# A linear attention and two feed-forward stages on one core: four small hand-overs between engines, a different order of preparation, and fewer fill products

## The chip, the cores and the metric

The kernel runs on one core of a Trainium2 chip. The metric is the device time of one execution in microseconds; the median of the runs counts. Five engines take part: TensorE (PE in the rows, PEld for its weight loads), VectorE (DVE), ScalarE (ACT), GpSimd (POOL), and SyncE (SP), which issues almost all DMAs.

## The reference

Three stages follow one another: a gated linear recurrence per batch and head, a feed-forward layer with a rational function of h, and a second feed-forward layer with a softmax-weighted, normalised h.

```python
for t in range(S):                       # B, H, S, D = 4, 8, 768, 48
    state = alpha[:, :, t, :, None] * state + einsum('bhd,bhe->bhde', k[:, :, t], v[:, :, t])
    y[:, :, t] = einsum('bhd,bhde->bhe', q[:, :, t], state)
h = x @ w_in                             # 3072 x 384, d_ff 2048
g = (a0 + a1*h + a2*h2 + a3*h3) / (1 + |b0||h| + |b1|h2 + 1e-6)
x = g @ w_out
h = x @ w_in                             # d_ff 1024
solu = h * softmax(h); out = layernorm(solu) * g_ln @ w_out
```

## The kernel before, in words

**Precision.** Every operand of the feed-forward products is split in two: `hi` is a copy rounded to float32r, `lo` the remainder, and each product is done three times (hi·hi, hi·lo, lo·hi).

**Halves.** The 768 steps are six chunks of 128. A chunk has two halves of two batches each; they are numbered 0 to 11 here, so the fourth half has the index 3 and the fifth the index 4. In a half the running product P of alpha and its inverse R are taken; q is multiplied by P and k by R; TensorE then forms the scores (`sc`, line 433), which ScalarE copies out of PSUM and GpSimd masks (lines 441, 442), the output `y` (458), and the state update `u` (498). At lines 485 and 486 y is split into the hi and lo parts of `xt`, the input of the first feed-forward layer: ScalarE copies hi, VectorE subtracts for lo.

**Preparing a half.** Halves 0 and 1 are prepared by `a_turn`: TensorE transposes alpha, k and q into PSUM (375), VectorE scans (386, 390) and multiplies k (394) and q (395). From half 2 on `a_dve` does it: VectorE transposes (302, 307, 336), scans (320, 329) and multiplies k (332), GpSimd multiplies q (347); the result goes out to HBM and comes back in another layout (`a_move_qk`, line 288). It is a generator with six steps.

**Units.** The first feed-forward layer is cut into 96 units, 16 per chunk (128 of its 2048 columns, 512 tokens). `m_up(u)` has nine products into a PSUM tile `hp` (line 607, three buffers, so unit u+3 waits until unit u is done with its tile), then a chain on ScalarE and VectorE (with `MIX` also on GpSimd: lines 625 to 631; without: 632 to 638). The last VectorE instruction of a unit is remembered as `fin[u]`. ScalarE makes `gh` (640), GpSimd `gl` (641). `m_down(u)`, four units later, has nine products into `x2p` (653). Of a unit with MIX VectorE has three instructions and GpSimd two more than without, where VectorE has four.

**Weights.** `w1_group(n)` loads and unpacks the float64 weights of units 4n to 4n+3 (and their second-layer rows) in seven steps; each step is one DMA, three VectorE instructions (552, 555, 556), one copy on ScalarE (562) and one subtraction on GpSimd (563). Groups 0 and 1 run ahead of the units, in buffers lent from later tiles; group 2 runs two steps per unit from unit 0, group 3 from unit 4.

**Order.** The order is written in the loop over u (from line 906): weights, fill products, `m_up(u)`, one step of the half in progress (`side`), `m_down(u-4)`. A planner orders the instructions of each engine by this program; `issue_after(x)` puts what it encloses behind instruction x in that order. `half_steps(i)` runs the scores, outputs and state update of half i (`a_pe`), one step per unit, and beside it two steps per unit of the preparation of half i+1, both behind `fin[u-2]` (`pin`, GP = GS = 2). A side is begun every eight units, at the units 2, 10, 18, ... (`LATE`).

**Fill products.** `busy(n, ins)` puts n bfloat16 products of zeros behind an instruction on TensorE (line 240). 66 of them lie at six places, 24 of these ahead of unit 3.

Of the kernel before, what the change touches and what calls it, by code (L numbers as in the profile page):

```python
# [7 lines left out]
F32 = mybir.dt.float32  # L8
# [22 lines left out]
def kernel(  # L31
# [32 lines left out]
    BUSY = {(0, 0): 14, (0, "kp", 1): 12, (1, 0): 4, (1, 1): 4, (1, "y"): 8, 3: 24}  # L64
# [15 lines left out]
    MIX = lambda u: u < 24 and u % 2 == 0  # L80
# [73 lines left out]
    def network(fast):  # L154
# [7 lines left out]
        if fast:  # L162
# [9 lines left out]
            zero = ap_.tile([128, CH], BF16, name="zero")  # L172
            nc.vector.memset(zero, 0.0)
# [3 lines left out]
            d1 = ap_.tile([128, NB6 * PER + 1], BF16, name="d1")  # L177
            d2 = ap_.tile([128, NB6 * PER], F32, name="d2")
# [6 lines left out]
        def clear():  # L185
            nc.gpsimd.memset(d1, 0.0)
            nc.gpsimd.memset(_view(d1[:], 0, [[PER, NB6 + 1]]), 1.0)
            nc.gpsimd.memset(d2, 0.0)
            nc.vector.memset(alT[:, 0:1], 0.0)
# [34 lines left out]
        halves = {}  # L224

# [6 lines left out]
        if fast:  # L232
            none = _view(zero[:], 0, [[0, NTOK // CH], [1, CH]])

        def busy(n, ins):
            if not spare:
                spare.append(ps_x2p.tile([128, NTOK], F32, name="spare", tag="x2p2"))
            with tc.issue_after(ins.ins):
                for _ in range(n):
                    nc.tensor.matmul(spare[0], lhsT=zero, rhs=none, start=True, stop=True)  # L240
# [124 lines left out]
        def a_turn(i):  # L365
# [15 lines left out]
            for p in range(2):  # L381
# [13 lines left out]
                marks[i, p, 0] = nc.vector.tensor_tensor(hf.q[p], turn(rq, p), P, ALU.mult)  # L395
# [28 lines left out]
        def a_pe(i):  # L424
# [58 lines left out]
            for z, n in enumerate((2, 1)):  # L483
                hi, lo = (xt[:, 2 * z:2 * z + n, w, 256 * bp:256 * bp + 256] for w in range(2))
                nc.scalar.activation(hi, y2[z], AF.Copy)
                marks[i, z] = nc.vector.tensor_tensor(lo, y2[z], hi.bitcast(F32), ALU.subtract)
# [35 lines left out]
        def split_w(src, hi, lo, scale=None):  # L522
# [16 lines left out]
            if src.dtype == I64:  # L539
# [8 lines left out]
                nc.sync.dma_start(out=st[:, :n], in_=src)  # L548
# [311 lines left out]
        def pin(n):  # L860
            stack = ExitStack()
            if n <= now[0] < NU and fast:
                for e, u in (("PE", now[0]), ("ACT", now[0] - n), ("POOL", now[0] - n)):
                    stack.enter_context(tc.issue_after(last[e, u].ins))
# [3 lines left out]
        def half_steps(i):  # L868
            gp = a_pe(i)
            gd = chain(a_prep(i + 1), a_move_qk(i + 1) if i + 1 >= NPE else iter(()), a_load(i + 2, ("ra", "rk")) if i + 2 < NH and i + 1 >= NPE else iter(())) if i + 1 < NH else iter(())  # L870
            while True:
                with pin(GP):
                    a = next(gp, "end")
                with pin(GS):
                    b = next(gd, "end")
                    if b != "end":
                        b = next(gd, "end")
                if a == "end" and b == "end":
# [11 lines left out]
        for u in range(NU + LAG):  # L890
            c, f = divmod(u, NF1)
            now[0] = u
            if f % (NF1 // 2) == LATE and u < NU:
# [3 lines left out]
            if u < NU:  # L897
# [7 lines left out]
                if fast and u < NF1:  # L905
# [6 lines left out]
                    with later(G1):  # L912
                        take(prep, 1)
# [3 lines left out]
                if fast and u < NF1:  # L917
                    with later(G1):
                        take(prep, 1)
# [157 lines left out]
```

## Time and profile before

| | us |
|---|---|
| median of 3 runs (lowest to highest) | 781.32 (779.75 to 789.72) |
| the profiled execution | 778.25 |
| span of its trace | 776.5 |
| TensorE, VectorE, ScalarE, GpSimd busy in the span | 737.9, 634.6, 534.1, 356.2 |
| mean granted clock of TensorE | 0.984 |

The times of the rows below are from the start of the span of the profiled execution. A granted clock of 1.00 is 2.4 GHz, of 0.50 1.2 GHz; a value between is a mean over a stretch with both.

### The profile page before, as it was taken

How to read it: one execution, taken by the hardware profiler on the slowest of the kernel's cores; microseconds unless marked ns; L12 is line 12 of the kernel's file. 1: busy time of each engine (PE TensorE's matmuls, PEld its weight loads, DVE VectorE, ACT ScalarE, POOL GpSimd, SP SyncE). 2: the span in 40 equal slices, each digit the busy share in tenths (PEclk: the TensorE clock that was granted, in tenths of full speed). 3: DMA queues.
4: the chain of work that ended last, by engine and by line, in shares of the span. 5: the costliest groups of instructions: out<-in, count | busy, mean ns of one | idle time of the engine just before them, and what ended most of it. 6: DMA issues, size and time to landing. Idle time of an engine off the chain costs nothing.

```text
span 776.5 us, 14048 instructions
## 1 busy us (share of the span) xinstructions
PE 737.9 (95%) x5042; PEld 605.7 (78%) x5042; DVE 634.6 (82%) x1110; ACT 534.1 (69%) x983; POOL 356.2 (46%) x306
## 2 busy tenths in 40 slices
PE   6788898999999999999999999999999999999996
PEld 4655676778887787778877788888888989989986
DVE  5999999999898989899898966568887697867630
ACT  2337856688878888788878887878865555555541
POOL 3256886577554355434444433422253333442322
PEclk9989997999999999999999999999999999999998
DMA  7997257376837383727545340820025353442552
GB/s 175 271 267 185 69 157 163 116 178 184 201 125 159 116 199 94 155 81 214 128 141 100 123 82 2 320 87 1 1 82 116 106 138 89 123 106 55 139 124 71
DMA packets 87278, 101.74 MB, mean 131 GB/s; under 512 B 34464, under 2 KB 63136, under 8 KB 87200
## 3 DMA queue, kind: packets, MB, share of 16 engines
q1 hardware_dynamic: 87104, 100.67, 49.2%
q8 instruction: 41, 0.67, 0.4%
q14 instruction: 37, 0.30, 0.1%
q10 hardware_dynamic: 96, 0.10, 0.0%
HBM read 60.59 MB, written 27.56 MB: 114 GB/s over the span
## 4 chain that ended last, share of the span: by engine, by line
PE 35%; DVE 20%; ACT 9%; issue 4%; DMA 2%; POOL 1%; SPq 1%; ACTq 0%; DVEq 0%; POOLq 0%
PE h L727 10%; PE op L791 9%; PE x2p L653 8%; PE hp L607 7%; DVE hp L637 2%; DVE p L633 2%; DVE w L636 2%; ACT hp L635 2%; DVE P L320 1%; DVE p L638 1%; DVE alT L336 1%; DVE room L767 1%; DVE qk L302 1%; ACT p L614 1%; ACT gh L640 1%
## 5 line engine op out<-in xcount | busy, mean ns | idle before, releaser
L607 PE MATMUL hp<-xt,g 128*128 128x512 f32 x864 | 222.5, 399 | 5.8 <-DVE alT L314 2.4
L641 POOL TENSOR_TENSOR gl<-p,gh 128x512 fp32r<-128x512 f32 x96 | 129.1, 1345 | 194.2 <-ACT gh L640 104.7
L653 PE MATMUL x2p<-gh,g 128*128 128x512 f32 x576 | 197.1, 396 | 2.1 <-ACT x2e L661 2.1
L607 PEld LDWEIGHTS hp<-xt,g 128*128 128x128 f32 x864 | 161.7, 190 | 45.7 <-DVE p L638 5.8
L653 PEld LDWEIGHTS x2p<-gh,g 128*128 128x128 f32 x576 | 108.0, 188 | 29.0 <-ACT x2e L661 4.7
L653 PE MATMUL x2p<-gl,g 128*128 128x512 f32 x288 | 113.7, 395 | 1.2 <-POOL gl L641 1.2
L791 PE MATMUL op<-w2oh,room 128*128 128x384 f32 x384 | 101.8, 339 | 1.5 <-ACT room L782 0.9
L783 POOL TENSOR_TENSOR room<-room,room 128x1024 fp32r<-128x1024 f32 x22 | 54.6, 2485 | 101.1 <-ACT room L782 96.6
L636 DVE SCALAR_TENSOR_TENSOR w<-w,co,hp 128x512 f32<-128x512 f32 x84 | 62.0, 738 | 42.0 <-ACT hp L635 41.0
L727 PE MATMUL h<-w2ih,x 128*128 128x512 f32 x288 | 90.8, 394 | 0.0
L614 ACT ACTIVATE p<-hp,co 128x512 f32<-128x512 f32 x96 | 65.9, 686 | 14.0 <-POOL gl L641 13.6
L635 ACT ACTIVATE hp<-ah 128x512 f32<-128x512 f32 x84 | 50.2, 597 | 33.9 <-DVE p L633 32.9
L791 PEld LDWEIGHTS op<-w2oh,room 128*128 128x128 f32 x384 | 70.1, 188 | 3.0 <-ACT room L782 1.2
L633 DVE SCALAR_TENSOR_TENSOR p<-p,co,hp 128x512 f32<-128x512 f32 x84 | 61.7, 734 | 10.4 <-ACT p L614 10.0
L615 ACT ACTIVATE w<-ah,co 128x512 f32<-128x512 f32 x96 | 69.4, 723 | 0.6 <-DVE p L631 0.2
L612 ACT ACTIVATE ah<-hp 128x512 f32<-128x512 f32 x96 | 56.6, 590 | 13.1 <-PE hp L607 12.6
L653 PEld LDWEIGHTS x2p<-gl,g 128*128 128x128 f32 x288 | 54.4, 189 | 13.9 <-POOL gl L641 1.6
L791 PE MATMUL op<-w2ol,room 128*128 128x384 f32 x192 | 65.0, 339 | 0.0
L640 ACT ACTIVATE gh<-p 128x512 fp32r<-128x512 f32 x96 | 59.9, 624 | 6.6 <-PE x2p L653 2.7
L727 PEld LDWEIGHTS h<-w2ih,x 128*128 128x128 f32 x288 | 53.9, 188 | 11.7
L638 DVE SCALAR_TENSOR_TENSOR p<-p,co,hp 128x512 f32<-128x512 f32 x84 | 62.0, 738 | 1.1
L634 ACT ACTIVATE ah<-w,co 128x512 f32<-128x512 f32 x84 | 60.6, 721 | 1.3
(170 smaller groups left out, 1281.1 us busy)
## 6 DMA issues: line engine op xcount, KB each, us to landing
room<-room SPq DMA_DIRECT2D x96, 128.0 KB, 2.3
qk_d<-qk SPq DMA_DIRECT2D x10, 771.0 KB, 4.9
st<-in_moe_w_in_dram SPq DMA_DIRECT2D x13, 512.0 KB, 4.7
st<-in_moe_w_out_dram SPq DMA_DIRECT2D x16, 384.0 KB, 4.5
qks<-qk_d SPq DMA_DIRECT2D x20, 257.0 KB, 5.1
x<-x_d SPq DMA_DIRECT2D x18, 256.0 KB, 3.2
out_dram<-o SPq DMA_DIRECT2D x94, 48.0 KB, 1.6
ra<-in_alpha_dram SPq DMA_DIRECT2D x44, 96.0 KB, 3.4
```

The lines of the kernel that those rows point to most:

```text
L607: last["PE", u] = nc.tensor.matmul(hp, lhsT=w[:, kt, 128 * o:128 * o + 128], rhs=xts[c][:, kt, xx, :], start=(kt == 0 and w is hi and xx = ...
L614: nc.scalar.activation(p, hp, AF.Square, bias=co[:, 7:8])
L615: nc.scalar.activation(w, ah, AF.Square, bias=co[:, 6:7])
L633: nc.vector.scalar_tensor_tensor(p, p, a1, hp, ALU.add, ALU.mult)
L635: nc.scalar.activation(hp, ah, AF.Exp, scale=-1.0)
L636: nc.vector.scalar_tensor_tensor(w, w, rest, hp, ALU.add, ALU.mult)
L638: fin[u] = nc.vector.scalar_tensor_tensor(p, p, a0, hp, ALU.add, ALU.mult)
L640: last["ACT", u] = nc.scalar.activation(gh, p, AF.Copy)
L641: last["POOL", u] = nc.gpsimd.tensor_tensor(gl, p, gh[:].bitcast(F32), ALU.subtract)
L653: nc.tensor.matmul(x2ps[c][d], lhsT=w[:, o, 128 * d:128 * d + 128], rhs=gg, start=(f == 0 and w is hi and gg is gh), stop=(f == NF1 - 1 an ...
L727: nc.tensor.matmul(hp[:, 512 * n:512 * n + 512], lhsT=x2s[c][:, kt, x, CH * b:CH * b + CH], rhs=w2[w][:, kt, 512 * n:512 * n + 512], start ...
L791: nc.tensor.matmul(op, lhsT=x[:, 128 * f:128 * f + 128], rhs=w2[w][:, f, :], start=(f == 0 and x is hi and w == "oh"), stop=(f == NF2 - 1 ...
```

## The change

It does the following. The q products of halves 0 and 1 go from one VectorE instruction each to a ScalarE copy out of PSUM and a GpSimd product. The lo part of y in halves 0 to 3 is formed by TensorE, which adds minus hi to y in PSUM (a product with a negated identity), and ScalarE copies the result. Units 0 and 2 lose MIX. The preparation of half 3 is held until unit 4 and that of half 4 until unit 13; the side of half 4 begins at unit 20 in place of 18. Group 2 takes no step in unit 0 and is put behind `fin[u-1]` in units 1 to 3; while `near` holds its loads are put behind the last load of group 1. The fill products become 50, 12 of them ahead of unit 3, and read the tile `d1`, which is now filled at the start and also gives the zeros of the scans.

```diff
-    BUSY = {(0, 0): 14, (0, "kp", 1): 12, (1, 0): 4, (1, 1): 4, (1, "y"): 8, 3: 24}
+    HOLD = {2: (4, 2), 3: (13, 2)}
+    BUSY = {(0, 0): 10, (0, "kp", 1): 8, (1, 0): 8, (1, 1): 8, (1, "y"): 4, 3: 12}
...
-    MIX = lambda u: u < 24 and u % 2 == 0
+    MIX = lambda u: 2 < u < 24 and u % 2 == 0
...
-            zero = ap_.tile([128, CH], BF16, name="zero")
-            nc.vector.memset(zero, 0.0)
+            minus = ap_.tile([128, 128], F32R, name="minus")
+            nc.scalar.activation(minus, ident, AF.Copy, scale=-1.0)
...
             d1 = ap_.tile([128, NB6 * PER + 1], BF16, name="d1")
+            nc.gpsimd.memset(d1, 0.0)
+            nc.gpsimd.memset(_view(d1[:], 0, [[PER, NB6 + 1]]), 1.0)
+            zero = d1[:, 1:1 + CH]
...
-            none = _view(zero[:], 0, [[0, NTOK // CH], [1, CH]])
+            none = d1[:, :NTOK]
...
-                    nc.tensor.matmul(spare[0], lhsT=zero, rhs=none, start=True, stop=True)
+                    nc.tensor.matmul(spare[0], lhsT=none[:, :128], rhs=none, start=True, stop=True)
...
-                marks[i, p, 0] = nc.vector.tensor_tensor(hf.q[p], turn(rq, p), P, ALU.mult)
+                nc.scalar.activation(hf.q[p], turn(rq, p), AF.Copy)
+                marks[i, p, 0] = nc.gpsimd.tensor_tensor(hf.q[p], hf.q[p], P, ALU.mult)
...
                 nc.scalar.activation(hi, y2[z], AF.Copy)
-                marks[i, z] = nc.vector.tensor_tensor(lo, y2[z], hi.bitcast(F32), ALU.subtract)
+                if i < NPE + 2:
+                    for a in range(n):
+                        nc.tensor.matmul(
+                            y2[z][:, a, :], lhsT=minus, rhs=hi[:, a, :], start=False, stop=True, skip_group_check=True
+                        )
+                    marks[i, z] = nc.scalar.activation(lo, y2[z], AF.Copy)
+                else:
+                    marks[i, z] = nc.vector.tensor_tensor(lo, y2[z], hi.bitcast(F32), ALU.subtract)
...
-                nc.sync.dma_start(out=st[:, :n], in_=src)
+                with tc.issue_after(sent["w"].ins) if stage["near"] else ExitStack():
+                    move = nc.sync.dma_start(out=st[:, :n], in_=src)
+                if stage["wide"]:
+                    sent["w"] = move
...
-                with pin(GS):
-                    b = next(gd, "end")
-                    if b != "end":
+                b = None
+                if now[0] >= HOLD.get(i, (0, 0))[0]:
+                    with pin(HOLD.get(i, (0, GS))[1]):
                         b = next(gd, "end")
+                        if b != "end":
+                            b = next(gd, "end")
...
-            if f % (NF1 // 2) == LATE and u < NU:
+            if f % (NF1 // 2) == (4 if u // (NF1 // 2) == 2 else LATE) and u < NU:
...
-                    with later(G1):
-                        take(prep, 1)
+                    with later(1 if u < 4 else G1):
+                        take(prep, 1 if u else 0)
```

The last pair stands twice, ahead of `m_up(u)` and behind it. `pin` takes the unit before where `m_up(u)` has not been written yet.

## Rows read from the trace of the kernel before

**Rows 1.** The page, busy time of each engine, share of the span, instructions

```profile
PE 737.9 (95%) x5042; PEld 605.7 (78%) x5042; DVE 634.6 (82%) x1110; ACT 534.1 (69%) x983; POOL 356.2 (46%) x306
```

**Rows 2.** Busy time by stretch: length, engines, TensorE clock, DMA share, GB/s

```profile
20.00:40.00 20.00, 16.02 (x207) 12.20 (x204) 19.53 (x56) 6.74 (x15) 6.75 (x8) 0.91 1.04 276
...
100.00:150.00 50.00, 45.33 (x388) 35.37 (x391) 48.66 (x71) 31.41 (x59) 35.48 (x31) 0.90 0.57 150
...
450.00:500.00 50.00, 50.00 (x366) 40.92 (x365) 32.38 (x46) 41.42 (x72) 16.87 (x17) 1.00 0.35 106
```

**Rows 3.** Chain that ended last, in order of time: nine of a unit's eighteen products

```profile
451.25 2.04 PE hp L607 x9
```

**Rows 4.** TensorE's timeline, first transposes, units 0, 3, 5, half 3's scores, unit 16

```profile
4.50 1.98 PE L375 MATMUL tp<-ident,ra 128*64 128x128 f32 x16 [4.50 <-POOL d L187]
...
55.20 1.04 PE L607 MATMUL hp<-xt,g 128*128 128x512 f32 x3
...
74.35 2.33 PE L607 MATMUL hp<-xt,g 128*128 128x512 f32 x9 [2.40 <-DVE alT L314]
...
85.35 2.34 PE L607 MATMUL hp<-xt,g 128*128 128x512 f32 x9 [1.03 <-DVE p L631]
...
120.62 2.03 PE L433 MATMUL sc<-qks 48*128 48x128 f32 x8 [1.70 <-DVE alT L314]
...
159.26 2.21 PE L607 MATMUL hp<-xt,g 128*128 128x512 f32 x9
```

**Rows 5.** VectorE's timeline, q products of halves 0 and 1 among others

```profile
16.56 0.69 DVE L395 TENSOR_TENSOR qks<-tp,Pp 128x512 f32<-128x512 f32 x1
17.61 0.69 DVE L552 TENSOR_SCALAR fp<-lent 128x512 int32<-128x512 int32 x1 [0.37 <-DMA lent<-in_moe_w_in_dram]
...
36.32 0.65 DVE L395 TENSOR_TENSOR lent<-tp,Pp 128x512 f32<-128x512 f32 x1
36.89 0.53 DVE L556 SCALAR_TENSOR_TENSOR ft<-lent,fp 128x384 int32<-128x384 int32 x1
```

**Rows 6.** Timelines of ScalarE and GpSimd: a copy from PSUM, an SBUF pair

```profile
43.28 0.58 ACT L441 ACTIVATE A<-sc 128x512 f32<-128x512 f32 x1
...
49.75 1.28 POOL L563 TENSOR_TENSOR g<-ft,g 128x512 fp32r<-128x512 f32 x1
```

**Rows 7.** The two splits of y of half 1: VectorE, then ScalarE

```profile
56.80 1.01 DVE L486 TENSOR_TENSOR xt<-y,xt 128x512 fp32r<-128x512 f32 x2
...
53.76 0.87 ACT L485 ACTIVATE xt<-y 128x512 fp32r<-128x512 f32 x2 [0.24 <-PE y L458]
```

**Rows 8.** VectorE's timeline up to the end of unit 0

```profile
63.89 0.71 DVE L552 TENSOR_SCALAR fp<-st 128x512 int32<-128x512 int32 x1
...
73.02 0.68 DVE L556 SCALAR_TENSOR_TENSOR ft<-lent,fp 128x512 int32<-128x512 int32 x1
73.61 0.68 DVE L631 SCALAR_TENSOR_TENSOR p<-w,hp 128x512 f32<-128x512 f32 x1
```

**Rows 9.** Instructions on tile alT, then on tile qk: length, VectorE, others

```profile
120.00:152.00 32.00, 10.01 (x10) 0.84 0.54 139
...
120.00:152.00 32.00, 7.40 (x13) 0.39 (x2) 0.41 (x1) 0.84 0.54 139
```

**Rows 10.** DMA issues from 0 to 60 us: KB each, us to landing

```profile
lent<-in_moe_w_out_dram SPq DMA_DIRECT2D x8, 384.0 KB, 6.3
```

**Rows 11.** TensorE's timeline: fill products at two granted clocks

```profile
49.34 1.89 PE L240 MATMUL spare<-zero 128*128 128x512 bf16 x4
...
68.75 3.20 PE L240 MATMUL spare<-zero 128*128 128x512 bf16 x14
```

**Rows 12.** GpSimd's timeline: the q product of half 3

```profile
105.72 1.82 POOL L347 TENSOR_TENSOR qk<-qk,P 128x768 f32<-128x768 f32 x1
```

**Rows 13.** VectorE's groups from 0 to 161 us: busy, mean ns

```profile
L555 DVE SCALAR_TENSOR_TENSOR ft<-st,ft 128x384 int32<-128x384 int32 (+1 forms) x7 | 7.0, 994 | 0.0
L555 DVE SCALAR_TENSOR_TENSOR fp<-st,fp 128x512 int32<-128x512 int32 (+1 forms) x10 | 6.4, 640 | 0.1
```

More of the change, by code (lines that the diff above doesn't have):

```diff
@@ L185, in clear @@
         def clear():
-            nc.gpsimd.memset(d1, 0.0)
-            nc.gpsimd.memset(_view(d1[:], 0, [[PER, NB6 + 1]]), 1.0)
             nc.gpsimd.memset(d2, 0.0)
@@ L224, in network @@
         halves = {}
+        sent = {}
         def half(i):
@@ L862, in pin @@
             if n <= now[0] < NU and fast:
-                for e, u in (("PE", now[0]), ("ACT", now[0] - n), ("POOL", now[0] - n)):
+                for e, u in (("PE", now[0] if ("PE", now[0]) in last else now[0] - 1), ("ACT", now[0] - n), ("POOL", now[0] - n)):
                     stack.enter_context(tc.issue_after(last[e, u].ins))
@@ L917, in network @@
                 if fast and u < NF1:
-                    with later(G1):
-                        take(prep, 1)
+                    with later(1 if u < 4 else G1):
+                        take(prep, 1 if u else 0)
             if u == NU:
```

## The prediction

> **What bounds the kernel now.** I read the page's busy times first, then the table by stretch, then the timelines of TensorE and VectorE up to 160 us. Over the whole span TensorE is busy 95% and VectorE 82% [rows 1], which hides two different stages. From 450 us on TensorE is busy 50.00 of 50 us while VectorE has 32.38 [rows 2]: TensorE is the bound, and a unit takes 2.04 + 2.04 = 4.08 us [rows 3]. In front it is the other way round: VectorE is busy 19.53 of 20 us between 20 and 40, and 48.66 of 50 between 100 and 150, where TensorE has 45.33 and a granted clock of 0.90 [rows 2]. Unit 0 begins at 55.20 and unit 16 at 159.26 [rows 4], so sixteen units take 104.1 us; at 4.08 each they need 65.3, beside the products of two halves of attention. Unit 3 stands for 2.40 us until VectorE's memset at line 314, which lies directly behind the end of unit 0, and unit 5 for 1.03 until unit 2 ends [rows 4]. So up to unit 16 what VectorE has to do sets the time, and from there TensorE. A microsecond that leaves VectorE's queue ahead of unit 16, or is put behind it, brings unit 16 forward by about one; after it nothing is gained.
>
> **The change part by part, as microseconds by which unit 16 comes earlier.**
>
> *q products.* Four VectorE instructions go. The next instruction starts 0.57 us after the one at 36.32 [rows 5], so 0.6 each, 2.4 in all. Behind the one at 16.56 VectorE waits 0.37 us for a weight DMA anyway [rows 5], so part of half 0's two is lost. Bounds 1.2 (half 1 alone) and 2.4; I take 1.8, the middle, since half 0 loses only a part. In their place come four ScalarE copies, by the copy of scores 0.58 us each, and four GpSimd products, by the subtraction of the same size 1.28 us each [rows 6]; in 20 to 40 us these engines are busy 6.74 and 6.75 of 20 [rows 2], and the copy does not have to wait for P, so both lie beside VectorE's scan and k product. Uncovered, half 1's chain would be longer by 0.58 + 1.28 − 0.65 = 1.2 us.
>
> *y splits.* VectorE gives up 0.6 + 0.35 = 0.95 us by the starts of the next instructions (0.68 and 0.41 by duration), and 0.92 at 56.80 [rows 7]: 1.9 for halves 0 and 1, and as much for halves 2 and 3, which also lie ahead of unit 16: 3.8. In place of it TensorE gets three products of 256 columns, by half of 2.04/9 us [rows 3] 0.34 us a half, which stand behind ScalarE's copy (0.87 us for two [rows 7]); then ScalarE copies twice more, 0.9 us. TensorE works its queue in order, so up to 0.87 + 0.34 = 1.2 us of it per half may be lost; in a stretch bound by VectorE that costs nothing, and I take nothing (bounds 0 and 4 × 1.2 = 4.8, the upper one only if nothing lies between). For half 1 it is even shorter: hi is ready at 54.63 and VectorE comes to lo at 56.80 only.
>
> *MIX off for units 0 and 2.* One VectorE instruction more each, of 0.68 us by the last of unit 0 [rows 8]: −1.3 (0 to −1.4). GpSimd loses two instructions per unit.
>
> *Group 2 behind unit 0.* Between 63.89 and 73.02 seven VectorE instructions of group 2, 0.6 us each, stand ahead of the end of unit 0 at 74.29 [rows 8]. They only move behind it, 4.2 us, so unit 0 ends near 74.3 − 3.7 − 4.2 + 0.7 = 67.1, and units 3 to 5 come earlier, but by unit 8 group 2 has to be there. As a sum over VectorE that is nothing. What it can cost: the step's DMA goes behind the same mark, and a load of this kind takes 6.3 us to land [rows 10]. With half 3's preparation held as well, VectorE may run dry there. Bounds 0 and −6.3; I take −2, nearer to 0, because the chains of units 1 and 2 lie ready. SP's order changes for these loads alone; behind them stand the reads of half 3's inputs, which are wanted later than before.
>
> *Half 3 from unit 4.* Moved, not removed, and its result is still wanted at unit 10: 0 here, and a rival below.
>
> *Half 4 from unit 13.* Its preparation is 10.01 + 7.40 us of VectorE, less about 2.6 for two lines that touch both tiles, 14.8 us, all of it between 120 and 152 [rows 9], that is ahead of unit 16. Held until unit 13, steps 1 and 2 stand behind the end of unit 11, 3 and 4 behind unit 12, 5 and 6 behind unit 13, and unit 16 waits for the end of unit 13 (three hp buffers). So the last two steps, about a quarter (3.7 us), surely fall behind it, and at most about 12 do. I take 6: the last two, and half of the two before. Unit 32 needs half 4, so the moved work has 16 units in which to be done, and the side of half 5 moves with it.
>
> *Fill products.* At full clock one takes 3.20/14 = 0.23 us, at 1.2 GHz 1.89/4 = 0.47 [rows 11]. Ahead of unit 3 twelve go (2.7 us), but TensorE stood 2.40 us behind them [rows 4], so nothing is gained. In half 1 eight are added and four go, +0.9 us at full clock, +1.9 at half, on the way from the scores to y; the larger number of them may in turn end the low clock earlier. Bounds −2 and +2, taken as 0.
>
> *Sum:* 1.8 + 3.8 − 1.3 − 2 + 6 = 8.3 us. Against the profiled execution: span 776.5 − 8.3 = 768.2, time 778.25 − 8.3 = 770.0. The median of the runs is 3.07 above that execution; 781.3 − 8.3 = **773.0 us**.
>
> **A rule against the change.** Line 555 takes 994 ns on average where both its inputs lie in SBUF, and 640 where one is in PSUM [rows 13]; GpSimd is at work beside both. The Trainium skill, page "SBUF — State Buffer", section "SBUF: two separate sides", says that VectorE, in an instruction with two SBUF inputs, and GpSimd share a pair of ports which one holds for its whole instruction while the other stands still. The trace agrees in the 994 against 640. The four new GpSimd products read SBUF. As a mechanism of this kernel: if VectorE stood still through each of them, 4 × 1.28 = 5.1 us come off, 8.3 − 5.1 = 3.2, and the time is 778.1. Against it: in halves 0 and 1 the scans, the k product and the unpacking of weights each read one operand from PSUM, so I give it a small chance.
>
> **The rivals.**
>
> *The order gives nothing.* If the planner or the waits let half 4's work be done ahead of unit 16 all the same, 6 us go: 8.3 − 6 = 2.3, 779.0 us. For it: VectorE's ready work is taken up wherever it waits a moment. Against: the pins are written out.
>
> *All of it moves, and no load is waited for.* 12 in place of 6, 0 in place of −2: 16.3, 765.0 us. For it: TensorE loses more than that ahead of unit 16 (104.1 against 65.3 and the attention). Against: steps 1 to 4 may run ahead of unit 13's end.
>
> *Half 3 comes too late (slower).* Its q product ends at 107.5 [rows 12], then its data go out to HBM and back, and at 120.62 the scores already stand 1.70 us on TensorE [rows 4], ahead of unit 11 in the queue. Now it starts behind unit 2's end in place of unit 0's: by the starts of units 5 and 3, 85.35 − 74.35 = 11.0 us later [rows 4]. If the whole of that comes through, −8.3 + 11.0 = +2.7, 784.0 us. It decides from where that product ends later than 107.5 + 8.3 = 115.8. Against it: group 2's and the units' work that stood beside it is then behind it no more, and VectorE's sum up to its end is the same or less.
>
> **How the numbers follow.** Forecast 0.45, order gives nothing 0.22, all moves 0.16, half 3 late 0.12, ports 0.05. The range from 764 to 784 holds the sum's own bounds and nearly all of the rivals; outside lie part of the 765 case (more than 16 us) and part of the late case (with a low clock on top), together under 0.2. The forecast's own range is 768 to 778. 2% is 15.6 us, about what a measurement of this kernel can tell from no change. Below 765.7 lies most of the third case: 0.13 for faster. Above 796.9 would need the late half twice over: 0.02. Between: 0.85.
>
> **What would show it.** Right: unit 0 begins near 51.5 in place of 55.20, unit 3 near 65 to 68, unit 16 near 151; VectorE's line 395 is gone and 486 begins with half 4; the scans of half 4 (lines 320 and 329) lie around the start of unit 16; behind unit 16 the distances between units are as before. Wrong: unit 16 within 3 us of 159; half 3's q product later than 115.8 and TensorE idle ahead of its scores; VectorE idle for more than 4 us between units 0 and 4 on weight loads; granted clock 0.5 for longer ahead of unit 16 than before, with TensorE waiting for nothing; or new TensorE gaps at the halves behind unit 20.

## The result, and the profile after

| | before | after |
|---|---|---|
| median of 16 runs each, us (lowest to highest) | 781.36 (777.0 to 789.72) | 791.08 (789.8 to 792.51) |
| ratio to before, 95% interval | | 1.0123 [1.0103, 1.0143] |
| profiled execution, span, us | 778.25, 776.5 | 792.39, 790.5 |
| mean granted clock | 0.984 | 0.976 |

The changed kernel is 9.7 us slower where 773.0 was forecast: outside the range, and with the other sign. The page of after, first line, answers to [rows 1]:

```profile
PE 740.8 (94%) x5033; PEld 610.6 (77%) x5038; DVE 631.5 (80%) x1099; ACT 539.3 (68%) x996; POOL 352.7 (45%) x306
```

VectorE does 3 us less, as meant. The next look is TensorE's timeline at four of the places of [rows 4]: first transposes, units 0, 3 and 16.

```profile
4.47 1.97 PE L378 MATMUL tp<-ident,ra 128*64 128x128 f32 x16 [4.47 <-POOL d L180]
...
65.15 0.86 PE L621 MATMUL hp<-xt,g 128*128 128x512 f32 x3
...
82.92 1.65 PE L621 MATMUL hp<-xt,g 128*128 128x512 f32 x3 [4.77 <-DVE p L652]
...
165.97 0.39 PE L621 MATMUL hp<-xt,g 128*128 128x512 f32 x1
```

The start is the same, unit 0 is 10.0 us late, unit 3 8.6, unit 16 6.7. Unit 32 begins at 251.0 in place of 241.2, and from there to unit 95 the lateness stays at 9.9. All of the loss lies ahead of unit 32. (The further 4.1 us of the profiled execution lie behind 730 us; before's profiled execution is 3.1 under its own median, and the medians differ by 9.7.)

The reading that sorts the rest is a sum for TensorE: up to the start of unit 32 the time is what TensorE was busy plus what it stood. The table by stretch of before, cut at units 0, 16 and 32 (columns as in [rows 2]):

```profile
0.00:55.20 55.20, 41.86 (x474) 31.05 (x475) 46.65 (x124) 17.55 (x41) 20.44 (x37) 0.91 0.89 238
55.20:159.30 104.10, 93.35 (x679) 70.86 (x678) 101.97 (x164) 70.62 (x131) 72.73 (x63) 0.95 0.52 143
159.30:241.20 81.90, 81.01 (x642) 65.19 (x641) 75.72 (x122) 68.38 (x124) 51.65 (x46) 1.00 0.68 169
0.00:241.20 241.20, 216.22 (x1791) 167.09 (x1792) 224.34 (x408) 156.55 (x293) 144.82 (x145) 0.96 0.66 174
```

and of after, cut at the same units:

```profile
0.00:65.20 65.20, 44.37 (x472) 33.03 (x477) 52.90 (x134) 23.12 (x51) 32.11 (x46) 0.90 0.83 223
65.20:166.00 100.80, 89.58 (x640) 70.35 (x641) 87.37 (x140) 71.40 (x134) 60.83 (x54) 0.92 0.44 119
166.00:251.00 85.00, 83.20 (x673) 67.10 (x672) 78.51 (x125) 66.86 (x123) 48.94 (x46) 1.00 0.66 181
0.00:251.00 251.00, 217.15 (x1781) 170.48 (x1787) 218.77 (x397) 161.38 (x306) 141.88 (x145) 0.94 0.62 167
```

TensorE stood 241.2 − 216.2 = 25.0 us before and 251.0 − 217.2 = 33.8 after: 8.9 of the 9.8 us are standing time. By stretch it is 13.3 to 20.8 ahead of unit 0 (+7.5), 10.8 to 11.2 up to unit 16, 0.9 to 1.8 up to unit 32. VectorE was busy 5.6 us less by unit 32 and it did not help. The 0.9 us of busy time hide a difference in the clock: by the lengths that the prediction used, 16 fill products fewer (0.23 each) and 12 products for y more (0.11 each) would make it 2.3 less, so some 3 us, an estimate, go with a mean clock of 0.94 in place of 0.96.

What TensorE waits for ahead of unit 0: first the list of before, then that of after (us in total, times, longest).

```profile
PE tp L375 <- POOL d L187: 4.5, 1, 4.5
PE tp L375 <- DVE Rp L390: 3.5, 3, 2.4
PE sc L433 <- ACT A L441: 2.1, 1, 2.1
PE tp L375 <- DVE co L129: 2.0, 1, 2.0
PE kp L404 <- DVE xt L486: 0.5, 1, 0.5
PE sc L433 <- DVE qks L394: 0.4, 1, 0.4
PE tp L375 <- DMA lent<-in_q_dram: 0.3, 1, 0.3
```

```profile
PE tp L378 <- POOL d L180: 4.5, 1, 4.5
PE tp L378 <- DMA lent<-in_alpha_dram: 4.0, 1, 4.0
PE y L462 <- POOL A L446: 3.7, 2, 2.5
PE kp L408 <- ACT xt L495: 2.0, 1, 2.0
PE tp L378 <- DVE Rp L393: 1.4, 1, 1.4
PE y L492 <- ACT xt L489: 1.1, 1, 1.1
PE spare L243 <- issue: 0.9, 4, 0.3
PE y L462 <- issue: 0.8, 1, 0.8
PE y L462 <- ACT A L445: 0.8, 1, 0.8
PE sc L437 <- ACT A L445: 0.7, 1, 0.7
PE tp L378 <- DMA rk<-in_k_dram: 0.7, 1, 0.7
PE tp L378 <- DMA lent<-in_q_dram: 0.2, 1, 0.2
```

Line by line: the transposes cost about the same (5.8 and 6.3, though a load has taken the place of two VectorE waits). New are 5.3 us in which `y` of half 1 waits for copied and masked scores (3.7 + 0.8, and 0.8 for which the profile names no cause, but which end at 53.20, just behind the third copy; the scores' own wait falls from 2.1 to 0.7, so +3.9 in all), 2.6 for the y split of TensorE (the product with `minus` waits 1.1 for ScalarE's hi, and `kp` 2.0 in place of 0.5 for ScalarE's lo), and 0.9 at fill products. Gone is 0.4, the scores' wait for VectorE's product (line 394). Together 0.5 + 3.9 + 2.6 + 0.9 − 0.4 = 7.5.

Why the scores are late is on ScalarE's timeline of after:

```profile
50.90 0.30 ACT L257 ACTIVATE jk<-qk,lim 128x6 f32<-128x6 f32 x1 [2.41 <-DVE qk L328]
...
51.98 0.63 ACT L576 ACTIVATE g<-ft 128x512 fp32r<-128x512 f32 x1 [0.69 <-DVE ft L570]
52.52 0.58 ACT L445 ACTIVATE A<-sc 128x512 f32<-128x512 f32 x1
56.21 0.63 ACT L576 ACTIVATE g<-ft 128x512 fp32r<-128x512 f32 x1 [3.11 <-DVE ft L570]
56.74 0.58 ACT L445 ACTIVATE A<-sc 128x512 f32<-128x512 f32 x1
```

Half 1's last scores left TensorE at 50.5. Their two copies stand behind half 2's watch (line 257) and two weight copies of group 1 (576), each of which waits for VectorE; they run at 52.52 and 56.74. Before, all four were done by 50.1, ahead of the watch. The code around them is the same in both; the order that the planner wrote for ScalarE is another. The same holds in part for the 2.6 us of the y split: by ScalarE's timeline of after, hi of half 1 starts at 64.18, 1.7 us after `y` is done, and lo of half 0 at 36.92, 1.4 us after the product with `minus`, in both cases behind weight copies that wait for VectorE, in half 0 also behind one of the new copies of q.

VectorE's timeline of after then shows the stand that follows from a late unit 0:

```profile
64.76 0.55 DVE L570 SCALAR_TENSOR_TENSOR ft<-lent,fp 128x384 int32<-128x384 int32 x1 [0.57 <-POOL g L577]
73.80 0.75 DVE L647 SCALAR_TENSOR_TENSOR p<-p,co,hp 128x512 f32<-128x512 f32 x1 [8.48 <-ACT p L628]
```

It stands 8.48 us for the first hp of unit 0. In the kernel before seven instructions of group 2 fill the wait for the end of unit 0, between 63.89 and 73.02 [rows 8].

### The profile page after: what moved, and what is told of

It reads as the page before. It is cut to its first block, busy times and chain, and to the rows that moved or that the text cites. A ratio compares the mean times of both kernels' runs of the same rounds, so it can differ in the third digit from the quotient of the medians.

```text
span 790.5 us, 14041 instructions
## 1 busy us (share of the span) xinstructions
PE 740.8 (94%) x5033; PEld 610.6 (77%) x5038; DVE 631.5 (80%) x1099; ACT 539.3 (68%) x996; POOL 352.7 (45%) x306
## 4 chain that ended last, share of the span: by engine, by line
DVE 38%; PE 21%; ACT 15%; DMA 9%; issue 7%; SPq 6%; POOL 3%; ACTq 0%; DVEq 0%; POOLq 0%
PE hp L621 8%; PE x2p L667 7%; SPq L791 3%; DVE room L781 3%; DVE hp L651 3%; DVE w L650 3%; DVE p L647 3%; DVE room L764 2%; PE op L805 2%; DMA rq<-in_q_dram 2%; ACT jk L766 2%; DVE room L779 2%; DVE p L652 2%; DVE sm L760 2%; ACT hp L649 2%
## 5 line engine op out<-in xcount | busy, mean ns | idle before, releaser
L655 POOL TENSOR_TENSOR gl<-p,gh 128x512 fp32r<-128x512 f32 x96 | 126.4, 1316 | 209.7 <-ACT gh L654 129.5
L647 DVE SCALAR_TENSOR_TENSOR p<-p,co,hp 128x512 f32<-128x512 f32 x86 | 63.3, 736 | 18.6 <-ACT p L628 18.3
L628 ACT ACTIVATE p<-hp,co 128x512 f32<-128x512 f32 x96 | 66.0, 688 | 11.0 <-POOL gl L655 10.8
L652 DVE SCALAR_TENSOR_TENSOR p<-p,co,hp 128x512 f32<-128x512 f32 x86 | 63.6, 740 | 1.1
```

The source lines that it names most:

```text
L628: nc.scalar.activation(p, hp, AF.Square, bias=co[:, 7:8])
L647: nc.vector.scalar_tensor_tensor(p, p, a1, hp, ALU.add, ALU.mult)
L652: fin[u] = nc.vector.scalar_tensor_tensor(p, p, a0, hp, ALU.add, ALU.mult)
L655: last["POOL", u] = nc.gpsimd.tensor_tensor(gl, p, gh[:].bitcast(F32), ALU.subtract)
```

## The experiments

Three theories stood at first. A: the loss is order, the score copies behind instructions that wait for VectorE. B: the loss is the held work, VectorE stands because group 2 and half 3 were put behind units. C: the loss is the longer chain of the y split through TensorE and ScalarE. Beside them stood what the prediction rests on, that VectorE's amount of work sets the time. This table is of all runs: the ratio of times, then from the profiled execution the start of unit 32, TensorE's busy and standing time and VectorE's busy time up to it, and TensorE's mean granted clock in that stretch (from the tables by stretch).

| kernel | median us, ratio [95%] | unit 32 | PE busy + standing | DVE | clock |
|---|---|---|---|---|---|
| before | 781.36 | 241.2 | 216.2 + 25.0 | 224.3 | 0.96 |
| after | 791.08, 1.0123 [1.0103, 1.0143] | 251.0 | 217.2 + 33.8 | 218.8 | 0.94 |
| e1 after, scores first | 786.06, 1.0061 [1.003, 1.0092] | 244.5 | 218.9 + 25.6 | 219.0 | 0.93 |
| e2 after, old order | 790.14, 1.0101 [1.0034, 1.0168] | 253.8 | 223.9 + 29.9 | 220.7 | 0.93 |
| e3 after, q on VectorE | 781.37, 0.9992 [0.9959, 1.0026] | 240.7 | 212.9 + 27.8 | 217.4 | 0.96 |
| e4 after, y on VectorE | 790.8, 1.013 [1.0058, 1.0202] | 248.7 | 215.2 + 33.5 | 217.6 | 0.95 |
| e5 before, q alone | 785.07, 1.0026 [0.9996, 1.0055] | 246.4 | 219.6 + 26.8 | 221.5 | 0.94 |
| e6 before, order alone | 786.37, 1.0065 [1.004, 1.009] | 245.2 | 216.2 + 29.0 | 220.4 | 0.96 |
| e7 before, y alone | 784.51, 1.0033 [1.0011, 1.0055] | 246.3 | 221.3 + 25.0 | 217.3 | 0.94 |
| e8 e1 with old fills | 783.82, 1.0027 [1.0001, 1.0054] | 246.9 | 221.4 + 25.5 | 220.2 | 0.94 |
| e9 before, two fills fewer | 778.66, 0.9949 [0.9922, 0.9976] | 241.0 | 216.0 + 25.0 | 222.3 | 0.95 |
| e10 before, four memsets | 782.88, 1.0001 [0.9969, 1.0034] | 241.5 | 213.0 + 28.5 | 225.5 | 0.97 |
| e11 before, new fills | 782.83, 0.9995 [0.9969, 1.0022] | 244.7 | 216.7 + 28.0 | 223.9 | 0.92 |
| e12 after, old q and fills | 783.33, 1.0003 [0.9981, 1.0026] | 242.9 | 218.7 + 24.2 | 219.9 | 0.94 |
| e13 before, half 4 alone | 780.82, 0.9996 [0.9968, 1.0024] | 240.1 | 214.3 + 25.8 | 222.1 | 0.97 |
| e14 before, more VectorE | 791.72, 1.0123 [1.0075, 1.0172] | 251.0 | 219.8 + 31.2 | 225.3 | 0.95 |
| e15 before, less VectorE | 779.1, 0.9953 [0.9919, 0.9987] | 240.4 | 214.4 + 26.0 | 212.3 | 0.96 |
| e16 e1, old order | 786.66, 1.0055 [1.0023, 1.0087] | 250.5 | 215.9 + 34.6 | 219.8 | 0.95 |
| e17 before, scores first | 782.83, 1.002 [0.9988, 1.0053] | 253.2 | 223.7 + 29.5 | 225.8 | 0.93 |
| e18 e14, scores first | 790.24, 1.0114 [1.0068, 1.016] | 248.7 | 217.2 + 31.5 | 226.6 | 0.95 |

A profiled execution is one of several. Those of e16 and e17 were late at unit 32 by 9.3 and 12.0 and made up 3 of it later, and e17's was 785.64 against a median of 782.83; where the two differ the median decides. Before's own profiled execution lies 3.1 us under its median, so 3 us at unit 32 against it say nothing about a kernel. The ratios are against executions of before that were timed along with each run; their medians were 781.31 to 782.77, so the medians of two rows are not to be subtracted.

### Order or held work: e1 and e2

e1 puts half 1's score copies ahead of the weight copies and of half 2's preparation on ScalarE:

```diff
-                    nc.scalar.activation(t, sc[j], AF.Copy)
+                    marks["A", i] = nc.scalar.activation(t, sc[j], AF.Copy)
...
-            take(pre, NA)
+            take(pre, 1)
+            with tc.issue_after(marks["A", 1].ins):
+                take(pre, NA - 1)
...
-            with tc.issue_after(marks[0, 1].ins):
+            with tc.issue_after(marks[0, 1].ins), tc.issue_after(marks["A", 1].ins):
                 _run(a_prep(2))
```

> The changed kernel, with ScalarE's copies for group 1 (all but its first step) and for half 2's preparation put behind ScalarE's last copy of half 1's scores. Theory A (the order on ScalarE: the last two copies of half 1's scores stand behind weight copies that wait for VectorE, so unit 0 begins at 65.2 in place of 55.2): unit 0 begins near 57, and the 8 us come back to the end, 782 to 784 us. Theory B (VectorE runs dry from 65 to 80 us, because group 2 and half 3 are held): unit 0 begins earlier, but VectorE still stands idle about 10 us between unit 0's start and the end of unit 0, and the time stays above 787. Theory C (the y split through TensorE and ScalarE is what delays): unit 0 stays near 63 and the time near 790.

e2 takes back the order: no half held, sides at units 2, 10, 18, group 2 as before.

```diff
-    HOLD = {2: (4, 2), 3: (13, 2)}
+    HOLD = {}
...
-                with tc.issue_after(sent["w"].ins) if stage["near"] else ExitStack():
+                with ExitStack():
...
-            if f % (NF1 // 2) == (4 if u // (NF1 // 2) == 2 else LATE) and u < NU:
+            if f % (NF1 // 2) == LATE and u < NU:
...
-                    with later(1 if u < 4 else G1):
-                        take(prep, 1 if u else 0)
+                    with later(G1):
+                        take(prep, 1)
```

> The changed kernel with the old order: group 2 from unit 0 and not pinned, halves 3 and 4 not held, side of half 4 at unit 18, loads not pinned. Theory A: unit 0 stays near 63 to 65 and the time near 788 or more. Theory B: VectorE is busy between 65 and 80 us, and the time comes back to 781 to 784, with unit 0 still late. Theory C: as A.

e1 gave back 5.0 us (1.0123 to 1.0061). Its ScalarE timeline has the last two copies at once, the later of them some 7.5 us earlier, and its table by stretch shows TensorE's standing time back at 244.5 − 218.9 = 25.6:

```profile
48.58 1.15 ACT L445 ACTIVATE A<-sc 128x512 f32<-128x512 f32 x2 [3.22 <-PE sc L437]
```

```profile
0.00:244.50 244.50, 218.91 (x1786) 172.33 (x1787) 218.96 (x397) 160.93 (x306) 141.30 (x145) 0.93 0.62 172
```

e2 gave back nothing that can be measured, and VectorE stands there just the same, with group 2 free to run. Its timeline:

```profile
72.01 0.69 DVE L566 TENSOR_SCALAR fp<-st 128x512 int32<-128x512 int32 x1 [7.94 <-ACT lent L413]
```

The first step of group 2 waits for the copy of half 1's `kp`, which is itself late. So B falls: the stand is a consequence of the late front. A is borne out for about half of the loss, with the reserve that 5.0 us is little more than the 4 us that an edit of next to no work moves below (e9). What e1 has left is not standing time but busy time, 218.9 us against 216.2, at a mean clock of 0.93 against 0.96. And what A names is still there at another place: in e1 hi of half 1 starts at 56.28, behind half 2's watch and two weight copies that wait for VectorE, 3.5 us after `y` is done, and TensorE stands 3.2 us for it. No run put that copy first.

### Which part, taken out or alone: e3 to e8

e3 gives q back to VectorE, e4 y (`if i < NPE + 2` becomes `if i < 0`); e5, e6 and e7 are the kernel before with q, with the order (HOLD, sides, group 2, loads, MIX) or with y alone, where `d1` is filled at the start as in after; e8 is e1 with before's fill products.

```diff
-                nc.scalar.activation(hf.q[p], turn(rq, p), AF.Copy)
-                marks[i, p, 0] = nc.gpsimd.tensor_tensor(hf.q[p], hf.q[p], P, ALU.mult)
+                marks[i, p, 0] = nc.vector.tensor_tensor(hf.q[p], turn(rq, p), P, ALU.mult)
```

> The changed kernel with the four q products back on VectorE. Theory A: the four score copies of half 1 stand with at most two weight copies and one watch between them, unit 0 begins near 58 to 60, time 784 to 786. Theory B: VectorE dry all the same, 789 to 792. Theory C: unchanged or 2 us slower, 790 to 793.

> The changed kernel with the four y splits back on VectorE. Theory C: unit 0 near 57 and the time 781 to 784. Theory A: unit 0 earlier by the 2 us that TensorE stood for the lo copy of half 0 only, time 787 to 790. Theory B: no gain, 790 to 793.

> Only the q products are moved (and d1 filled at the start); y splits, order, MIX and fill products as before. In this program ScalarE's last three copies of half 1's scores stand together, ahead of the second weight copy of group 1. Theory A (the order on ScalarE, which the move of q brings about only together with other edits, is what costs): unit 0 begins within 2 us of 55.2 and the time is 779 to 783. Rival Q (the products on GpSimd and the copies on ScalarE cost by themselves, by ports or by a longer chain): unit 0 near 58 or later, unit 32 later by 3 or more, time 785 or more.

> Only the order is changed: group 2 behind unit 0, half 3 held to unit 4, half 4 to unit 13, side of half 4 at unit 20, MIX off for units 0 and 2, loads of group 2 pinned; q, y and the fill products as before. By the sum of the prediction: +6 for half 4, -2 for loads, -1.3 for MIX, so unit 16 is 3 us earlier and stays so, 778 to 779. Rival D (what is put off must be done before unit 32, in which TensorE then waits): unit 16 is 3 to 6 us earlier, unit 32 within 1 us of before, time 780.5 to 783.

> Only the four y splits are moved to TensorE and ScalarE; all else as before. By the sum of the prediction 3.7 us are gained: 777 to 779. Rival Y (the second pair of copies on ScalarE and TensorE's wait for the first make the chain of halves 0 and 1 longer by as much as VectorE gains): TensorE's wait ahead of half 0's kp products grows from 0.5 to 1.5 us or more, unit 0 no earlier than 55, time 780 to 784.

> Scores first as in e1, with the 66 fill products of before in their old places. Theory K (what is left of the loss in e1, 786.06, is the low clock: 34 us of it ahead of unit 32 against 20 before): low clock falls to about 20 us, time 782 to 784. Theory Q (the move of q costs by itself): low clock falls or not, the time stays at 785 to 787.

The move of q is the part on which the loss hangs: e3, with all the rest of the change in it, is level with before. Yet alone (e5) it costs 0.26%, within its interval of nothing. e4 shows no gain or loss from y within the change, e7 0.33% alone; e6 0.65%. So C falls too, though in e4 unit 0 begins at 58.1, 7.1 us ahead of after and near what C expected: 2.3 us of that lead are left at unit 32, and the time is that of after. Three parts that were each to gain do not gain by themselves, and two of them lose. Their costs do not add up: that 0.26, 0.65 and 0.33% make 1.24% and the change costs 1.23% is a coincidence, for y and the order together, without q (e3, and e12 with the old fills), are level and not 0.98% slower. e8's 1.0027 lies below e1's 1.0061, and its time is the one that theory K named, but the intervals overlap and its mean clock up to unit 32 is 0.94 and not the 0.96 of before: how much of e1's rest is the clock's is not settled.

Two of these show where a gain failed to come. In e7 VectorE does 7 us less up to unit 32 than before, TensorE stands exactly as long (25.0), and is busy 5.1 us longer:

```profile
0.00:246.30 246.30, 221.30 (x1803) 171.20 (x1804) 217.26 (x399) 159.72 (x302) 144.54 (x145) 0.94 0.62 169
```

Twelve more products (1803 against 1791) are 1.4 us of it, by 0.11 each at full clock; the rest goes with the clock, 0.94 against 0.96. In e5 unit 0 begins 2.5 us earlier, but TensorE has stood 13.5 us by then, as before (13.3); the gain was a higher clock (0.97 against 0.91), and by unit 15 it is 6.9 late.

```profile
0.00:52.70 52.70, 39.24 (x475) 29.20 (x475) 42.70 (x118) 20.35 (x46) 24.81 (x42) 0.97 0.90 243
```

### How much is chance of the order: e9 to e12

e9 takes two of the 66 fill products away, e10 adds a memset of one column to each of four steps of VectorE, e11 makes the fill edit alone, e12 undoes q and the fills in the changed kernel.

```diff
-    BUSY = {(0, 0): 14, (0, "kp", 1): 12, (1, 0): 4, (1, 1): 4, (1, "y"): 8, 3: 24}
+    BUSY = {(0, 0): 12, (0, "kp", 1): 12, (1, 0): 4, (1, 1): 4, (1, "y"): 8, 3: 24}
```

```diff
+                nc.vector.memset(ap_.tile([128, 1], F32, name="nil", tag="nil"), 0.0)
```

> The kernel before with 12 in place of 14 fill products behind half 0's first scores, where TensorE stands 2.0 us afterwards anyway. By its work this edit is worth nothing. Theory P (ahead of unit 16 the order that the planner writes into each engine's queue decides, and any edit in front makes it write another order): the orders on ScalarE and VectorE differ from before, and the time differs from before by 2 to 6 us, more likely upward. Rival N (the order is robust, and only the work and its waits count): within 1.5 us of before, 780 to 783.

> The kernel before with a VectorE memset of one column (0.06 us) behind each of the four q products. By its work 0.24 us of VectorE. Theory P: 2 to 6 us off before. Rival N: 0 to 0.5 us slower, 781 to 783.

> The kernel before with the 50 fill products of the change in their places and nothing else. The prediction priced this at 0 (bounds -2 and +2). Theory F (12 products fewer ahead of unit 3 and 8 more in half 1 cost by themselves, by low clock and a longer way to y): unit 0 later by 1 to 2 us, time 783 to 785. Theory P: off by 2 to 6 us either way, with the place of the loss not at the fill products. Rival N: 780 to 783.

> The changed kernel with the q products on VectorE and the 66 fill products in their old places: y splits, order and MIX changed. e3, with the new fill products, took 781.37. Additive from the single edits (y +3.2, order +5.1 over before): 789. Theory A (only the moved q spoils the order on ScalarE): 779 to 783. Theory P: anywhere between 778 and 788, not to be had by adding the parts.

Two products fewer, some 0.5 us of work, moved the median by 4.1 us; four memsets more moved it by nothing, and so did sixteen products fewer (e11). So an edit of next to no work was worth some 4 us in one case, and nothing in others. The traces tell e9 and e10 apart: in e10 ScalarE and GpSimd run the same instructions in the same order as before, and VectorE too but for the four memsets; in e9 instructions stand at other places on all three engines, from the first 25 us on. But another order alone does not decide it, for e11's is another as well and its time is level. Theory P named the size of e9 and held the other sign for more likely; in e10 its premise, that any edit in front changes the order, fails. e9 is the fastest kernel of the study; its profiled execution is only 0.2 us ahead at unit 32, so where it gains is not shown.

### Half 4 alone, and VectorE's work from both sides: e13 to e15

e13 holds half 4's preparation to unit 13 and begins its side at unit 20, in the kernel before (with `d1` filled at the start):

```diff
+    HOLD = {3: (13, 2)}
...
-            if f % (NF1 // 2) == LATE and u < NU:
+            if f % (NF1 // 2) == (4 if u // (NF1 // 2) == 2 else LATE) and u < NU:
```

> The kernel before, with one part of the order alone: the preparation of half 4 held until unit 13 and its side begun at unit 20. In front the queues stay nearly as they were. The prediction's term: unit 16 comes 6 us earlier and so does everything behind it, time 775 to 777. The rival, that the work is paid back before unit 32, which needs half 4: unit 16 comes 3 to 6 us earlier, unit 32 within 1.5 us of 241.2, time 780 to 784.

It is level, as the rival said, but not by the way that it named. Its table by stretch up to units 0 and 16:

```profile
0.00:55.87 55.87, 41.82 (x474) 31.00 (x475) 45.73 (x122) 17.72 (x41) 19.92 (x37) 0.94 0.87 239
55.87:157.96 102.09, 91.69 (x679) 69.32 (x678) 98.33 (x159) 72.62 (x133) 73.78 (x63) 0.97 0.47 128
```

VectorE is busy 144.1 us ahead of unit 16 in place of 148.6, and unit 16 begins only 1.3 us earlier, where the term said 6 and the rival 3 to 6. Unit 22 then begins 6.0 us earlier, unit 32 1.1. Between 16 and 32 TensorE hardly stands longer (it is busy 80.8 of 82.1 us); the scores, outputs and state update of half 4 merely lie behind those units in its queue now, so the lead at unit 22 is no gain.

e14 makes the lo subtraction of y twice, e15 leaves the instruction of line 555 out in groups 2 and 3 (their weights then lack their highest bits):

```diff
+                if i < NPE + 2:
+                    marks[i, z] = nc.vector.tensor_tensor(lo, y2[z], hi.bitcast(F32), ALU.subtract)
                 marks[i, z] = nc.vector.tensor_tensor(lo, y2[z], hi.bitcast(F32), ALU.subtract)
```

```diff
-                nc.vector.scalar_tensor_tensor(gi, w32[:, :, 1], -0x40000000, gi, ALU.bitwise_and, ALU.bitwise_or)
+                if x < 14 or x > 27:
+                    nc.vector.scalar_tensor_tensor(gi, w32[:, :, 1], -0x40000000, gi, ALU.bitwise_and, ALU.bitwise_or)
```

> The kernel before, in which VectorE makes the four lo subtractions of y of halves 0 to 3 twice over, with the same result: 8 instructions at 0.68 us by length, 3.8 by the prediction's starts, all of it ahead of unit 16. If VectorE's sum sets the time there, unit 32 comes 3.8 us later and the time is 785 to 786. If it does not, unit 32 comes 0 to 2 us later, time 780 to 784; more than 6 us would be the planner's order again.

> The kernel before, without the instruction of line 555 in the fourteen weight steps of groups 2 and 3 (left out is the highest bits of those weights, their signs among them): by 640 to 994 ns each, 9 to 14 us of VectorE less, all of it between units 0 and 8. If VectorE's sum sets the time up to unit 16, unit 16 comes at least 6 us earlier and the time is 771 to 776. If what is freed is used up by other waits before unit 32, unit 32 comes 0 to 3 us earlier, time 778 to 782.

The table by stretch of e15, cut at units 0 and 16, and its total up to unit 32:

```profile
0.00:57.15 57.15, 42.15 (x475) 31.59 (x475) 44.77 (x122) 17.22 (x40) 19.25 (x37) 0.94 0.85 226
57.15:159.55 102.40, 92.10 (x677) 70.94 (x677) 93.69 (x155) 71.49 (x134) 75.94 (x65) 0.93 0.61 157
...
0.00:240.40 240.40, 214.39 (x1790) 167.87 (x1791) 212.34 (x394) 156.04 (x293) 144.90 (x145) 0.96 0.66 175
```

Ahead of unit 16 VectorE is busy 138.5 us in place of 148.6, and unit 16 begins at 159.55, 0.3 us later. Up to unit 32 it is 212.3 in place of 224.3, TensorE stands 26.0 in place of 25.0, and unit 32 begins 0.8 us earlier. By the ratio 0.47% come back, 0.81% at the most, where 12 us would be 1.5%: VectorE's amount of work does not set the time one for one. In e14 1.0 us more of busy VectorE by unit 32 went with 9.8 us: what counts is not how much, but where it stands.

### Order or place: e16 to e18

In e14 the planner had again put the last two score copies behind half 2's watch; there, though, they waited for the scores themselves and not for the watch (1.75 and 0.42 us for TensorE). e17 and e18 are before and e14 with e1's pin; e16 is e1 with e2's edit.

> The changed kernel with ScalarE's copies of half 1's scores first, as in e1_scores_first, and in it the edits of the order undone: group 2 as before, nothing held, sides at units 2, 10, 18, loads of group 2 free. Kept are q, y, MIX and fills. If the rest of e1's loss (about 4 us at unit 32) comes from the edits of the order, unit 32 comes near 241 and the time is 780 to 783. If it comes from the hand-overs themselves, it stays at 785 to 787.

> The kernel before with ScalarE's copies of half 1's scores put ahead of its weight copies of group 1 (all but the first step) and of half 2's watch, as in e1; nothing else. Before already has three of the four copies ahead of them. If the place of these copies on ScalarE is what the front hangs on, little is left to gain here: unit 0 at 53 to 56, time 780 to 783. It is the base for the next run.

> e14 (four lo subtractions made twice, 3.8 us more of VectorE) with the same pin as e17. If e14's 10 us came mostly from two score copies that the planner put behind half 2's watch, this run is 5 us or more faster than e14, 783 to 787, with unit 0 at 55 to 59. If they came from the work on VectorE itself, it stays at 789 to 793.

e16 stays where e1 is, so what is left of e1's loss is not in the held work. e17 is level with before, as expected (its unit 0, at 57.5, later than expected). e18 is not: with the score copies first (all by 52.6) it is still 1.14% slower, so in e14 and e18 theory A is not the cause. TensorE's list of waits of e18 names it:

```profile
PE kp L404 <- DVE xt L488: 9.9, 2, 5.6
```

The same wait was 1.8 us in two before. Behind `y` come hi on ScalarE, lo on VectorE, then `kp`, which takes its place in PSUM from the same buffers; the doubled subtractions lie on that chain with VectorE's scan and k product between them (58.64 to 64.48 in half 1 in place of 56.80 to 57.8 [rows 7]). They cost by their place in VectorE's queue, and not by their length.

## Why the prediction was wrong

**The step that failed is the base of the sum**: "up to unit 16 what VectorE has to do sets the time", and a microsecond that leaves its queue there "brings unit 16 forward by about one". Busy shares of 98% were read as a bound. e15 takes 10 us out ahead of unit 16, which does not come earlier, and gains 0.47% by the runs; e13 moves 4.5 behind it and gains nothing, e7 takes out 7 by unit 32 and loses 0.33%. It seems that VectorE is full there because ready work is plentiful (weights, the next half), not because all of it is wanted next; no run tests this reading by itself. What had to be read is TensorE's list of waits up to unit 32, which adds up to 24.5 of the 25.0 us before and, at the same clock, holds about the most that each part could return. Behind the rows shown above, these are the ones that bear on the change:

```profile
PE hp L607 <- DVE alT L314: 2.4, 1, 2.4
...
PE kp L404 <- DVE xt L486: 1.8, 2, 1.3
PE sc L433 <- DVE alT L314: 1.7, 1, 1.7
PE hp L607 <- DVE p L638: 1.5, 1, 1.5
PE u L498 <- DVE xt L486: 1.3, 2, 0.9
```

For q there is 0.4 (the scores' wait for line 394) and, if VectorE's scan comes sooner, a part of the 3.5 in which the transposes wait for it; that wait fell to 1.4 in after and 2.5 in e5, but the transposes then waited 4.0 and 2.7 for half 1's alpha. For y there is 1.8 + 1.3 = 3.1 in four halves, for the ends of units 2.4 + 1.5 + 1.0. Against these small sums stood new steps on ScalarE and GpSimd.

**q products (+1.8 forecast).** The four instructions went, as said, and the cover by ScalarE's and GpSimd's idle shares held for their lengths. Not priced was that four copies more on ScalarE change its order. Within the change this part costs 1.3% (e3 against after), about half of it, as far as e1 shows, by the order of the score copies. Where the other half comes from is open; e8 leaves room for a part by the fills and the clock, and e1's wait for hi of half 1 for a part by ScalarE's order.

**y splits (+3.8).** The chain through ScalarE, TensorE and ScalarE was bounded by 0 and 4.8 and taken as 0, "a stretch bound by VectorE". Ahead of unit 0 it measured 2.6 (1.1 and 1.5): the upper end, for two halves, in part because the new copies stand behind weight copies on ScalarE. Alone it costs 0.33% (e7).

**MIX (−1.3)** was tried only together with the order (e6), so its term is open.

**Group 2 (−2, for loads).** VectorE did stand, 8.48 us, but on unit 0's first hp and not on a load, and it stands 7.94 with the edit undone (e2). The mark of that step holds VectorE's instructions alone; that the DMA goes "behind the same mark" was misread, its place comes from the loads of group 1: in after the first load of group 2 has landed by 62, and VectorE takes it up at 82.8.

**Half 4 (+6).** It measures 1.3 at unit 16, 1.1 at unit 32 and nothing by the ratio (e13). "Moved behind unit 16" was counted as gained. Between 120 and 160 us TensorE stood only 3.1 us before (busy 17.86 and 19.02 of two 20 us), so, at the clock of that stretch, no deferral of VectorE work could give 6 there; and with the whole order (e6) unit 16 does come 5.5 earlier, and TensorE then stands 7.3 us between it and unit 32, where it stood 0.9.

**Fill products (0).** Right: 0.9995 (e11).

**The rivals.** "Half 3 too late" had its step right and its price wrong. Its q product begins at 116.74 in place of 105.72 [rows 12], the 11.0 us named, and ends past the mark of 115.8; but its scores, at 136.30 in place of 120.62, begin without a wait where they stood 1.70 before, and the 1.5 us that TensorE stands ahead of the next ones have no cause named in the profile. So its data were late and TensorE had other products to do; no loss of the named size went by way of half 3. "The order gives nothing" came nearest in mechanism, and could not reach the size. Signs that were named as wrong came: unit 16 not ahead, half 3's q product later than 115.8, VectorE idle over 4 us between units 0 and 4 (but not on a load), more time at the low clock (0.90 and 0.92 in the first two stretches against 0.91 and 0.95). The range was too narrow because each term was bounded by itself, in work moved, and none held what a different order of the queues does; e9 came out 4 us off for an edit of next to no work.

## What to carry to other kernels

When an engine is full in a stretch, ask whether the engine that ends last there waits for it: its list of waits, added up, is about the most that relief can return at the same clock, and a part that relieves no line of that list has nothing to gain from, however much work it moves. In a stage where several in-order queues hand work to one another, price an edit by where its new instructions fall in each queue, and look which short copies on the critical hand-over stand behind something that waits for a third engine. With an automatic order, time a few edits of no size first: their scatter is what a single small gain has to beat.

## What the runs showed of the hardware

In after a scan of VectorE and a mask of GpSimd of half 1's scores fall together; the two rows are from the timelines of VectorE and GpSimd.

```profile
53.00 2.59 DVE L332 TENSOR_TENSOR_SCAN alT<-alT,d 128x774 f32<-128x774 f32 x1
```

```profile
52.70 1.27 POOL L577 TENSOR_TENSOR g<-ft,g 128x512 fp32r<-128x512 f32 x1 [2.75 <-ACT g L576]
53.92 2.10 POOL L446 TENSOR_SCALAR_AFFINE_SELECT A<-A 128x512 f32<-128x512 f32 x1
```

Undisturbed the scan takes 1.74 and the mask 0.64. The scan starts during a GpSimd subtraction that ends at 53.97, and 0.97 + 1.74 = 2.7 is about its 2.59; the mask starts during the scan, which ends at 55.59, and 1.67 + 0.64 = 2.3 is near its 2.10. Each seems to run only when the other is done. `y` waited for that mask until 56.08, some 1.5 us longer for it, but this by itself did not delay unit 0: the last products of `y` waited until 59.28 in any case, for the mask of the copy at 56.74. The scan's 0.9 us (2.59 − 1.74) reach further, by the rows: VectorE's next instruction, at 55.52, is the one for which ScalarE's weight copy at 56.21 waits, ahead of that last score copy. The Trainium skill, page "SBUF — State Buffer", section "SBUF: two separate sides", says that the ports shared by GpSimd and a VectorE instruction with two SBUF inputs are held exclusively for a whole instruction; the rows agree. The four new GpSimd products, for which the prediction weighed that rule, took 1.19 to 1.28 us each and were not held up.

TensorE's mean clock has a price that can be read across runs with the same 1791 products up to unit 32: 213.0 us busy at 0.97 (e10), 216.2 at 0.96 (before), 219.6 at 0.94 (e5). A hundredth of mean clock went with about 2 us of busy time, as much as any single term of the forecast but two.

Half 1's alpha, 96 KB, landed 8.0 us after its issue in after and 4.8 in before, with the issue at the same time (12.37 and 12.38) and the same loads issued ahead of it in the same order. The change is not what made it late: in e9 and e17, which load in that order too, it took 7.5 and 8.2 (issued at 12.16 and 11.40), in e10 5.7. What sets it is open.
